# Weights' sums and low parts on VectorE, the keys' copy as a DMA, and matmuls of zeros ahead of the dense units

## The chip, the cores and the metric

The kernel runs on one core of one Trainium2 chip. The metric is device microseconds from the start to the end of one launch. TensorE multiplies 128x128 blocks into PSUM banks; VectorE (DVE in the profile), ScalarE (ACT) and GpSimd (POOL) are the elementwise engines; DMAs are issued by SyncE (SP), and a few by ScalarE. Each engine runs its own queue in order and waits on semaphores.

## The reference

Causal attention with decay (4 batches, 8 heads, 576 positions, head size 64), then two dense layers of 2304 tokens, 512 to 2048 to 512, one with the square of relu and one with elu between its matrices:

```
decay = cum[:, :, :, None] - cum[:, :, None, :]          # cum: running sum of log f
attn  = softmax(where(causal, -1e9, q @ k.T / 8 + decay))
x = (attn @ v) as 2304 x 512
x = relu(x @ w_in) ** 2 @ w_out                          # first layer (w1)
y = elu(x @ w_in2) @ w_out2                              # second layer (w2)
```

All is float32. The kernel splits each operand of a product into a high part, which a matmul takes in one pass, and a low part, the rest, and adds three matmuls: high by high, low by high, high by low.

## The kernel before

**Attention with dense units between.** Batch 0 runs with plain float32 operands (`Plain`); its A items (queries 0 to 255) come first for all heads, then the others. Batches 1 to 3 are loaded per head by `load_head` with part "F": ScalarE copies queries and keys to `qk1` (high parts), GpSimd makes the queries' low part in `qk2` and the keys' low part in the lower half of `qk1` (`ql`, `kl`, line 132), VectorE copies the keys' high part from `qk1` to `qk2` (`kh` is "v" for F, line 127), and a small DMA brings the rows of the decay (line 319). A head is loaded two items ahead of its use. While attention runs, `moe_step` puts pieces of six dense units (256 tokens each, half of the first layer's hidden units) between its steps; `fill` pays out credit for them and does nothing until the tokens of unit 0 and their weights are there. Weights come as raw 64-bit words, 16 tiles for the first units; `words` turns a tile into float32 with one ScalarE operation and four VectorE operations (lines 150 to 154), and a ScalarE copy and a subtraction give high and low parts.

**First layer's rest.** `first_layer(j)` runs blocks of 512 tokens in the order 3, 4, 0, 1, 2 (block 4 has 256). Per hidden chunk it makes 12 matmuls of 512 columns to `pH`, then relu (ACT), square (VectorE, line 573), high part (ACT, 574), low part (VectorE, 119), and 12 more matmuls to the four banks `O`, up to two chunks later. At a block's end VectorE adds `pr` and `operands` makes seven combinations of the block for the second layer with ACT, GpSimd (`yl` line 132, sums line 822) and VectorE, and stores them.

**Second layer.** It multiplies 2x2 blocks with seven products instead of eight, so the weights too need sums. `pair_weights(p)` prepares a pair of hidden chunks: four raw tiles through `words`, four sums of 128x256 (`add`, line 915) and seven high and low parts of 128x256 (`op`: ACT line 911, then `less` on GpSimd, line 132, tile `v`), and after a `yield` each, two high and low parts of 128x512 (ACT line 933, GpSimd line 132). Eight pairs exist. Pairs 0 to 3 are made while blocks 0, 1 and 2 of the first layer run (3, 4 and 5 of the 12 pieces), pair 4 in steps 4 to 6 of the second layer, pairs 5 to 7 from step 16 on (`w_at`: 2, 3, 2, 2 pieces after steps 18 to 21). A step is one block by one pair; steps 20 to 23 use pairs 4 to 7 for the first time. `first_product` makes seven products of six matmuls of 256 columns into four banks `P`, which ACT (line 995) and VectorE (lines 998, 1016) take out; then elu (1012, 1017 minimum; 1020 exp; 1021) and the low part (1024); `second_product` of the step before adds 24 matmuls of 512 columns.

The order of each engine's queue is fixed when the program is built, by a scheduler that lays the instructions out by its own estimates of time; so a change of engine also moves instructions that the code does not touch.

Of the kernel before, what the change touches and what calls it, by code (L numbers as in the profile page):

```python
# [10 lines left out]
F32 = mybir.dt.float32  # L11
F32R = mybir.dt.float32r
# [31 lines left out]

PLAIN_B = 4
CP = {'pA': 'a', 'pB': 'av', 'xA': 'a', 'xB': 'a'}
ENG = {'qk': 'aaa', 'ql': 'ppp', 'kh': 'pvv', 'kl': 'ppp', 'vh': 'ppp', 'vl': 'ppp', 'xl': 'pv'}
NORM = 'ap'
GL = 'pv'
SQ = 'appp'  # L50
# [4 lines left out]


OPS = 7
AUG0 = 2
AUG1 = 8
AUG_AT = 3  # L60
# [9 lines left out]
def f32(ap):  # L70
    return ap.bitcast(F32)
# [10 lines left out]
def attention_then_moe_kernel(ctx, tc, first, firstv, plain, qkv, aug0, f, w1, w2, out):  # L82
    nc = tc.nc
# [5 lines left out]
    const = pool(ctx, "const", 1, "left")  # L89
# [17 lines left out]
    def mask(ap, pat):  # L107
        nc.gpsimd.affine_select(out=ap, in_=ap, pattern=pat, compare_op=ALU.is_ge, fill=-8.0e9, base=0, channel_multiplier=1)
# [3 lines left out]
    seen = [None]  # L112
    trail = []

    def minus(eng, dst, x, hi):
        if eng == "p":
            less(dst, x, hi)
        else:
            nc.vector.tensor_tensor(dst, x, f32(hi), op=ALU.subtract)  # L119
# [11 lines left out]
    def less(dst, x, hi):  # L131
        nc.gpsimd.tensor_tensor(out=dst, in0=x, in1=f32(hi), op=ALU.subtract)  # L132
# [66 lines left out]
    ps_h = pool(un, "ps_h", 1, "left", space=PS)  # L199
# [37 lines left out]
    nc.gpsimd.memset(m4, 0.0)  # L237
    for k in range(2):
        mask(m4[64 * k:64 * k + 64, 224:288], [[-1, 64]])

    raws = {}

# [397 lines left out]
    def interleave(main, n_main, side, n_side):  # L640
        done = 0
        for i, _ in enumerate(main):
            while done * n_main < (i + 1) * n_side:
                if next(side, "end") == "end":
                    break
                done += 1
        return done
# [36 lines left out]
    started = [False] * NU  # L684
# [31 lines left out]
    for i in range(len(todo) + LAG):  # L716
        if i == AUG0:
            nc.sync.dma_start(out=aug[0:H], in_=aug0[0:H])
        if i == AUG1:
            nc.sync.dma_start(out=aug[H:], in_=aug0[H:])  # L720
        if i == AUG_AT:
            cpn = aug_split()
            aug_rows(slice(0, H), *cpn)
        if i == AUG1:
            aug_rows(slice(H, B * H), *cpn)
        while fetches and fetches[0][0] <= i + FETCH:
            fetch_head(*fetches.pop(0)[1:])
        if i == 0:
            for _ in range(5):
                stage()  # L730
        while loads and loads[0][0] <= i + AHEAD:
            load(*loads.pop(0)[1:])
        if i < len(todo):
            sg = soft(*todo[i])
            b, hp, kind, k = todo[i]
        else:
            sg = iter(())
        if i >= LAG:
            o = todo[i - LAG]
            og = outs(*o)  # L740
        else:
            o, og = None, iter(())
        for _ in range(W_AT[i] if i < len(W_AT) else 0):
            next(wl, None)
        n_moe = PACE[b] * COST[kind]
        n_out = {"A": 3, "4": 1, "B": 8}[o[2]] if o else 1
        n_steps = n_out + 1
        done = 0
        step = 0

        def fill():
            nonlocal done, step, credit
            step += 1
            trail.append(seen[0])
            credit += n_moe / n_steps
            while credit >= 1:
                credit -= 1
                if not moe_step():
                    credit = min(credit, 1.0)
                    break  # L760

        drain(sg)
        fill()
        for _ in og:
            fill()
        if o and o[2] in "AB" and o[3]:
            stored[o[0]] += 1
# [76 lines left out]
    def first_layer(j, nxt):  # L844
        t0, n = blocks[j]
        whole = t0 >= NU * CH
        x = xq.pop(j)
        if nxt is not None:
            fetch1(nxt)
        pr = xa.tile([128, NC, 512], F32, tag="xu", name="pr")  # L850
        if not whole:
            for i in range(n // CH):
                nc.sync.dma_start(out=pr[:, :, i * CH:(i + 1) * CH], in_=part[t0 // CH + i])
        po = [ps_O.tile([128, 512], F32, tag=f"O{c}", name=f"O{c}") for c in range(NC)]
        f0 = 0 if whole else 8

        def second_b(fc, gh, gl):
            for c in range(NC):
                mm3(po[c][:, 0:n], three([wout(1, fc, t, c) for t in range(2)], [gh[:, 0:n], gl[:, 0:n]]), fc == f0, fc == 15)

        pend, depth = [], DEPTH1 * 512 // n
        for fc in range(f0, 16):
            ph = h_tile()
            for c in range(NC):
                mm3(ph[:, 0:n], three([win(1, fc, t, c) for t in range(2)], [x[c][:, 0], x[c][:, 1]]), c == 0, c == NC - 1)
            g = relu2(ph, n, GL[1], "v")
            pend.append((fc, *g))
            if len(pend) > depth:
                second_b(*pend.pop(0))
            yield  # L870
        for p in pend:
            second_b(*p)
        for c in range(NC):
            y = pr[:, c, 0:n]
            if whole:
                nc.vector.tensor_copy(y, po[c][:, 0:n])
            else:
                nc.vector.tensor_tensor(y, po[c][:, 0:n], y, op=ALU.add)
        operands(j, pr)
        yield  # L880
# [23 lines left out]
    def pair_weights(p):  # L904
        wi = [w_tile([128, 4, 2, 256]), w_tile([128, 3, 2, 256])]
        wo = w_tile([128, 2, 2, 512])
        wp[p] = wi, wo

        def op(a, k):
            h, l = (wi[k // 4][:, k % 4, r] for r in range(2))  # L910
            nc.scalar.activation(out=h, in_=a, func=AF.Copy)  # L911
            less(l, a, h)

        def add(out, x, y, f):
            nc.gpsimd.tensor_tensor(out=out, in0=x, in1=y, op=f)  # L915

        ta, tb = (next_w() for i in range(2))
        a11, a12, a21, a22 = (t[:, c:c + 256] for t in (ta, tb) for c in (0, 256))
        op(a11, 0)
        op(a12, 5)  # L920
        op(a22, 4)
        add(a22, a21, a22, ALU.add)
        add(a21, a11, a21, ALU.subtract)
        add(a11, a22, a11, ALU.subtract)
        add(a12, a12, a11, ALU.subtract)
        op(a22, 3)
        op(a21, 2)
        op(a11, 1)
        op(a12, 6)
        yield  # L930
        for i in range(2):
            t = next_w()
            nc.scalar.activation(out=wo[:, i, 0], in_=t, func=AF.Copy)
            less(wo[:, i, 1], t, wo[:, i, 0])
            yield

    def fetch2(j, ks):
# [133 lines left out]
    ask_w()  # L1071
    wl2 = chain(pair_weights(p) for p in range(8))
    interleave(first_layer(0, 1), 9, wl2, 3)
    interleave(first_layer(1, 2), 9, wl2, 4)
    fetch2(4, range(0, 2))
    for i, _ in enumerate(first_layer(2, None)):
        if i in (3, 4, 5, 6, 7):
            next(wl2)
    fetch2(4, range(2, 3))
    fetch2(3, range(0, 6))  # L1080
# [73 lines left out]
```

## Time and profile before

| | us |
|---|---|
| median of 3 runs | 1055.4 (1054.61 to 1058.65) |
| profiled execution, its own time | 1054.71 |
| its span | 1052.7 |
| PE busy in the span | 1010.2 (96%) |
| DVE, ACT, POOL busy | 691.1, 545.8, 375.4 |

A matmul's end is modelled, so a matmul that waits for nothing seems to overlap the next one, and PE's busy share hides short pauses. Where starts matter, the distance from one matmul to the next is used. The column PEclk is the granted share of TensorE's clock, of 2.4 GHz; half of it is 1.2 GHz. Ahead of the first record of a change the column reads 1.00.

### The profile page before, as it was taken

To read this page: it belongs to the slowest core of one execution; us is meant where nothing else is said; L and a number is where in the kernel's file an instruction comes from. 1 tells how busy PE (TensorE), PEld (TensorE's weight loads), DVE (VectorE), ACT (ScalarE), POOL (GpSimd) and SP (SyncE) were. 2 spreads that over 40 slices of the span, in tenths; PEclk is the share of its full clock that TensorE was granted. 3 is DMA by queue.
4 is the path that set the end of the run, shared out by engine and by line. 5 is a ranking of instruction groups with operands and counts; after the bars stand their busy time and mean duration, and the time that the engine had idled before them with its cause. 6 is when DMAs were issued, how large, how long until landed. Compare 5 with 4: busy or idle time off the path is not lost.

```text
span 1052.7 us, 17378 instructions
## 1 busy us (share of the span) xinstructions
PE 1010.2 (96%) x6272; PEld 889.1 (84%) x6272; DVE 691.1 (66%) x1462; ACT 545.8 (52%) x1218; POOL 375.4 (36%) x400
## 2 busy tenths in 40 slices
PE   5899999999999999999999997999999999999998
PEld 3577788999999988889988775898988888899987
DVE  5993587776776548845467858695555878655554
ACT  4865688877886634424343434454334555333331
POOL 3556587576774300012144565440000445000000
PEclk9999999999999999999999999999999999999999
DMA  8843444543431074442645545625315365444502
GB/s 248 240 145 134 153 138 142 181 137 128 160 120 45 33 253 138 122 138 103 201 142 204 193 158 178 225 85 196 132 48 180 124 217 166 134 151 122 169 21 80
DMA packets 71960, 154.91 MB, mean 147 GB/s; under 512 B 8932, under 2 KB 34276, under 8 KB 71844
## 3 DMA queue, kind: packets, MB, share of 16 engines
q1 hardware_dynamic: 71812, 153.75, 44.8%
q8 instruction: 49, 0.80, 0.3%
q14 instruction: 35, 0.29, 0.1%
q10 hardware_dynamic: 64, 0.07, 0.0%
HBM read 115.15 MB, written 39.22 MB: 147 GB/s over the span
## 4 chain that ended last, share of the span: by engine, by line
PE 59%; issue 16%; DVE 12%; POOL 5%; ACT 4%; DMA 3%; SPq 0%; POOLq 0%; ACTq 0%; DVEq 0%
PE O L183 18%; PE pH L183 9%; PE P L183 8%; PE o L183 6%; PE ph L183 6%; PE pt L405 4%; PE pv L412 3%; DVE wt L153 2%; POOL v L132 2%; PE s L337 2%; PE s L338 2%; DVE wt L151 1%; POOL wt L915 1%; DVE wt L152 1%; PE pv L409 1%
## 5 line engine op out<-in xcount | busy, mean ns | idle before, releaser
L183 PEld LDWEIGHTS P<-xu,v 128*128 128x128 f32 x1536 | 200.3, 189 | 12.9 <-ACT hs L995 2.7
L183 PE MATMUL P<-xu,v 128*128 128x256 f32 x1536 | 203.5, 283 | 3.2 <-ACT hs L995 2.5
L183 PE MATMUL O<-v,gh 128*128 128x512 f32 x576 | 172.5, 395 | 0.6 <-ACT gh L966 0.5
L132 POOL TENSOR_TENSOR v<-wt,v 128x256 fp32r<-128x256 f32 (+1 forms) x72 | 72.5, 1015 | 211.7 <-ACT v L911 155.9
L183 PE MATMUL pH<-xu,w 128*128 128x512 f32 (+1 forms) x672 | 140.7, 360 | 0.0
L183 PEld LDWEIGHTS pH<-xu,w 128*128 128x128 f32 x672 | 114.0, 188 | 20.1
L183 PE MATMUL O<-gh,w 128*128 128x512 f32 (+1 forms) x448 | 122.8, 363 | 5.1 <-ACT gh L574 5.1
L183 PEld LDWEIGHTS O<-v,gh 128*128 128x128 f32 x576 | 103.4, 189 | 19.0 <-ACT gh L966 0.7
L995 ACT ACTIVATE hs<-P 128x256 f32<-128x256 f32 x128 | 47.9, 380 | 114.1 <-PE P L183 113.7
L183 PE MATMUL O<-v,gl 128*128 128x512 f32 x288 | 104.2, 394 | 0.5 <-DVE gl L988 0.5
L183 PEld LDWEIGHTS O<-gh,w 128*128 128x128 f32 x448 | 79.7, 189 | 19.9 <-ACT gh L574 6.2
L132 POOL TENSOR_TENSOR qk<-raw,qk 64x704 fp32r<-64x704 f32 (+1 forms) x48 | 78.9, 1643 | 20.4 <-ACT qk L123 15.2
L183 PE MATMUL O<-gl,w 128*128 128x512 f32 (+1 forms) x224 | 80.4, 365 | 3.9 <-DVE gl L119 3.9
L998 DVE TENSOR_TENSOR hs<-P,hs 128x256 f32<-128x256 f32 x96 | 40.4, 421 | 64.3 <-PE P L183 62.6
L132 POOL TENSOR_TENSOR yl<-pr,yh 128x512 fp32r<-128x512 f32 x18 | 24.7, 1371 | 158.7 <-ACT yh L815 108.2
L183 PE MATMUL o<-gh,w 128*128 128x256 f32 x384 | 76.6, 292 | 1.2 <-DVE xB L437 1.2
L150 ACT ACTIVATE wt<-wraw 128x512 f32<-128x512 f32 x57 | 38.2, 671 | 61.6 <-DMA wraw<-in_w_dram 38.6
L574 ACT ACTIVATE gh<-g 128x512 fp32r<-128x512 f32 (+1 forms) x80 | 46.8, 585 | 43.0 <-DVE g L573 39.1
L183 PE MATMUL ph<-xu,w 128*128 128x256 f32 x480 | 67.2, 287 | 1.3 <-DMA xu<-x 1.0
L1024 DVE TENSOR_TENSOR gl<-g,gh 128x512 fp32r<-128x512 f32 x64 | 47.3, 738 | 28.4 <-ACT gh L966 27.9
L573 DVE TENSOR_TENSOR g<-g 128x512 f32<-128x512 f32 (+1 forms) x56 | 45.4, 810 | 28.3 <-ACT g L569 28.2
L183 PEld LDWEIGHTS O<-v,gl 128*128 128x128 f32 x288 | 53.3, 188 | 11.6 <-DVE gl L988 0.8
(151 smaller groups left out, 2122.7 us busy)
## 6 DMA issues: line engine op xcount, KB each, us to landing
xu<-x SPq DMA_DIRECT2D x66, 512.0 KB
wraw<-in_w_dram SPq DMA_DIRECT2D x57, 512.0 KB
raw<-in_qkv_dram SPq DMA_DIRECT2D x24, 800.0 KB
x<-yh SPq DMA_DIRECT2D x31, 256.0 KB
x<-yl SPq DMA_DIRECT2D x31, 256.0 KB
x<-xs SPq DMA_DIRECT2D x16, 320.0 KB
xu<-x SPq DMA_DIRECT2D x16, 256.0 KB
raws_w<-in_w_dram SPq DMA_DIRECT2D x7, 512.0 KB
```

The source lines that it names most:

```text
L132: nc.gpsimd.tensor_tensor(out=dst, in0=x, in1=f32(hi), op=ALU.subtract)
L150: nc.scalar.activation(out=f32(t), in_=f32(hi), func=AF.Abs)
L153: nc.vector.scalar_tensor_tensor(t, hi, -0x40000000, t, op0=ALU.bitwise_and, op1=ALU.bitwise_or)
L183: nc.tensor.matmul(out=dst, lhsT=l, rhs=r, start=first and i == 0, stop=last and i == n - 1, skip_group_check=skip)
L337: nc.tensor.matmul(out=dst, lhsT=qk1[:, q0:q0 + 128], rhs=qk1[:, QW + j0:QW + j0 + n], start=first, stop=False)
L405: seen[0] = nc.tensor.transpose(dst, src, ident[:, c0:c0 + 128])
L412: seen[0] = nc.tensor.matmul(out=dst, lhsT=hh[2][:, J, :], rhs=hl[i], start=first and i == 0, stop=last and i == 1)
L573: (nc.vector if sq == "v" else nc.gpsimd).tensor_tensor(out=g[:, 0:n], in0=g[:, 0:n], in1=g[:, 0:n], op=ALU.mult)
L574: nc.scalar.activation(out=gh[:, 0:n], in_=g[:, 0:n], func=AF.Copy)
L995: nc.scalar.activation(out=o, in_=x, func=AF.Copy)
L998: nc.vector.tensor_tensor(o, y, x, op=ALU.add)
L1024: nc.vector.tensor_tensor(hl[i][1], gs[i], f32(hl[i][0]), op=ALU.subtract)
```

## The change

- `add` and the two `less` in `pair_weights` go from GpSimd to VectorE: per pair 4 sums and 7 low parts of 128x256, and 2 low parts of 128x512.
- Of the 12 pieces of pairs 0 to 3, block 1 gets 3 in place of 4, block 2 gets 6 in place of 5, the first at its first chunk.
- The keys' high part of batches 1 to 3 is copied from `qk1` to `qk2` by a DMA on SyncE's queue ("d"); the branch was there already.
- VectorE zeroes a tile of 128x128 at the start, and TensorE multiplies zeros into the units' bank `h` (256 columns each): 60 at once, and after each step of attention until unit 0 begins, 2 or 3 behind the last attention matmul, 59 in all.

```diff
-ENG = {'qk': 'aaa', 'ql': 'ppp', 'kh': 'pvv', ...}
+ENG = {'qk': 'aaa', 'ql': 'ppp', 'kh': 'pvd', ...}
...
+WARM, FILL, FILL_TO = 60, 2, 14
...
+    zero = const.tile([128, 128], F32R, name="zero")
+    nc.vector.memset(f32(zero), 0.0)
+    idle = ps_h.tile([128, 512], F32, tag="h", name="idle")
+
+    def busy(n):
+        for _ in range(n):
+            nc.tensor.matmul(out=idle[:, 0:256]..., lhsT=zero, rhs=zero.unsqueeze(1).broadcast_to([128, 2, 128]), start=True, stop=True)
+
+    busy(WARM)
...
+            went = False
             while credit >= 1:
                 credit -= 1
                 if not moe_step():
                     credit = min(credit, 1.0)
                     break
+                went = True
+            if not started[0] and not went and i < FILL_TO:
+                with tc.issue_after(seen[0].ins):
+                    busy(FILL + (step == 1))
...
         def op(a, k):
             h, l = (wi[k // 4][:, k % 4, r] for r in range(2))
             nc.scalar.activation(out=h, in_=a, func=AF.Copy)
-            less(l, a, h)
+            minus('v', l, a, h)
 
         def add(out, x, y, f):
-            nc.gpsimd.tensor_tensor(out=out, in0=x, in1=y, op=f)
+            nc.vector.tensor_tensor(out, x, y, op=f)
...
-            less(wo[:, i, 1], t, wo[:, i, 0])
+            minus('v', wo[:, i, 1], t, wo[:, i, 0])
...
-    interleave(first_layer(1, 2), 9, wl2, 4)
+    interleave(first_layer(1, 2), 9, wl2, 3)
     fetch2(4, range(0, 2))
     for i, _ in enumerate(first_layer(2, None)):
-        if i in (3, 4, 5, 6, 7):
+        if i in (0, 3, 4, 5, 6, 7):
             next(wl2)
```

Line numbers after the change are 13 to 18 higher from line 245 on. TensorE's queue at the start of the program, before (`s` scores, `pt` transposed weights of attention, `pv` their product with values):

```order
L333 MATMUL s<-rawA 128x256 x6
L405 MATMUL pt<-ident,ea 128x128 x4
L333 MATMUL s<-rawA 128x256 x2
L405 MATMUL pt<-ident,ea 128x128 x2
L409 MATMUL pv<-ea,rawA 64x256
L409 MATMUL pv<-ea,rawA 64x128
L405 MATMUL pr<-ident,rb 128x128 x2
```

The same place after the change (`idle` is the bank that the zeros go to):

```order
L250 MATMUL idle<-zero 128x256 x60
L346 MATMUL s<-rawA 128x256 x2
L250 MATMUL idle<-zero 128x256 x3
L346 MATMUL s<-rawA 128x256 x2
L250 MATMUL idle<-zero 128x256 x3
L346 MATMUL s<-rawA 128x256 x2
L418 MATMUL pt<-ident,ea 128x128
L346 MATMUL s<-rawA 128x256 x2
L418 MATMUL pt<-ident,ea 128x128 x2
L250 MATMUL idle<-zero 128x256 x2
```

The zeros stand ahead of the first scores and between the steps that follow. SyncE's queue where heads of batch 1 are loaded, before (319 decay rows, 448 a store of attention's result, 251 a head's fetch, 593 a unit's tokens):

```order
L319 DMA qk_1440<-aug 4x1280
L319 DMA qk_1704<-aug 4x1280
L448 DMA x_0_70<-xs 128x2x320
L251 DMA raw<-in_qkv_dram 128x1600
L593 DMA xu<-x_0_70 128x2x256
```

After (335 is the new copy of keys):

```order
L332 DMA qk_1562<-aug 4x1280
L335 DMA qk_1562<-qk_1561 64x576
L332 DMA qk_1826<-aug 4x1280
L461 DMA x_0_70<-xs 128x2x320
L335 DMA qk_1826<-qk_1825 64x576
L264 DMA raw<-in_qkv_dram 128x1600
```

The second copy stands behind a store and ahead of a head's fetch. VectorE's queue from the minimum of step 22 on, before (151 to 154 are `words`):

```order
L1012 TENSOR_SCALAR g<-hs 128x512
L1016 TENSOR_TENSOR hs<-hs 128x256
L1021 SCALAR_TENSOR_TENSOR g<-g,hs 128x512
L1024 TENSOR_TENSOR gl<-g,gh 128x512
L998 TENSOR_TENSOR hs<-P,hs 128x256
L1017 TENSOR_SCALAR g<-hs 128x512
L151 TENSOR_SCALAR wt<-wt 128x512
L998 TENSOR_TENSOR hs<-P,hs 128x256
```

The second half of the same step after the change (122 with `v` is a low part of a weight, 933 a sum of weights, 1042 and 1016 are 1024 and 998 of before):

```order
L1039 SCALAR_TENSOR_TENSOR g<-g,hs 128x512
L122 TENSOR_TENSOR v_10040<-wt,v_10040 128x256
L933 TENSOR_TENSOR wt<-wt 128x256
L1042 TENSOR_TENSOR gl<-g,gh 128x512
L933 TENSOR_TENSOR wt<-wt 128x256
L122 TENSOR_TENSOR v_10039<-wt,v_10039 128x256
L933 TENSOR_TENSOR wt<-wt 128x256
L122 TENSOR_TENSOR v_10039<-wt,v_10039 128x256
L933 TENSOR_TENSOR wt<-wt 128x256
L122 TENSOR_TENSOR v_10039<-wt,v_10039 128x256
L1016 TENSOR_TENSOR hs<-P,hs 128x256
```

Pair 7's sums and low parts now stand in VectorE's queue between a step's elu and the next addition.

## Rows read from the trace of the kernel before

**Rows 1.** Windows by stage: length, busy (count) per engine, granted clock, DMA share, GB/s.
```profile
12.70:24.00 11.30, 11.29 (x33) 7.94 (x33) 6.83 (x24) 7.12 (x20) 3.51 (x4) 1.00 0.84 259
24.00:60.00 36.00, 30.64 (x132) 18.80 (x132) 34.06 (x91) 28.89 (x78) 18.51 (x21) 0.95 0.86 240
...
120.00:220.00 100.00, 96.03 (x729) 89.66 (x728) 76.81 (x233) 83.09 (x208) 72.89 (x79) 1.00 0.45 149
...
600.00:680.00 80.00, 70.45 (x350) 57.38 (x349) 56.77 (x80) 34.64 (x67) 46.26 (x42) 1.00 0.59 210
...
820.00:900.00 80.00, 76.22 (x460) 67.44 (x459) 67.09 (x114) 43.13 (x93) 36.38 (x39) 0.98 0.55 183
```

**Rows 2.** Chain that ended last: start, us, what.
```profile
141.27 2.87 PE ph L183 x24
...
404.19 2.76 PE O L183 x12
```

**Rows 3.** Groups by form, 600 to 680 us: two that TensorE waits in.
```profile
L183 PE MATMUL O<-gh,w 128*128 128x512 f32 x72 | 22.5, 400 | 5.1 <-ACT gh L574 5.1
...
L183 PE MATMUL O<-gl,w 128*128 128x512 f32 x36 | 14.3, 411 | 3.9 <-DVE gl L119 3.9
```

**Rows 4.** Groups by form, 820 to 900 us: all matmuls.
```profile
L183 PE MATMUL P<-xu,v 128*128 128x256 f32 x295 | 40.1, 286 | 3.2 <-ACT hs L995 2.5 <-DVE hs L998 0.6
L183 PE MATMUL O<-v,gh 128*128 128x512 f32 x112 | 33.1, 406 | 0.6 <-ACT gh L966 0.5
L183 PE MATMUL O<-v,gl 128*128 128x512 f32 x53 | 18.0, 395 | 0.0
```

**Rows 5.** Groups by form, whole run: GpSimd on the weights.
```profile
L132 POOL TENSOR_TENSOR v<-wt,v 128x256 fp32r<-128x256 f32 x56 | 51.0, 921 | 158.3 <-ACT v L911 155.9 <-PE pH L183 2.4
...
L915 POOL TENSOR_TENSOR wt<-wt 128x256 f32<-128x256 f32 x32 | 27.5, 860 | 1.3
...
L132 POOL TENSOR_TENSOR v<-wt,v 128x512 fp32r<-128x512 f32 x16 | 21.5, 1344 | 53.4 <-ACT v L933 53.4
```

**Rows 6.** VectorE by line: ns least/median/most, first and last start.
```profile
L1016 DVE TENSOR_TENSOR hs<-hs x32: 411/424/1502, 688.8 to 1019.1; 128x256 f32<-128x256 f32 x32
L153 DVE SCALAR_TENSOR_TENSOR wt<-wraw,wt x57: 668/692/1793, 24.3 to 890.3; 128x512 int32<-128x512 int32 x57
L119 DVE TENSOR_TENSOR w<-wt,w x16: 681/684/694, 385.3 to 447.9; 128x512 fp32r<-128x512 f32 x16
L127 DVE CAST qk<-qk x24: 442/480/1923, 87.4 to 318.1; 64x576 fp32r<-64x576 f32 x24
```

**Rows 7.** VectorE's groups by form, 600 to 680 us.
```profile
L119 DVE TENSOR_TENSOR gl<-g,gh 128x512 fp32r<-128x512 f32 x9 | 8.6, 953 | 5.4 <-ACT gh L574 5.4
```

**Rows 8.** VectorE's groups by form, 820 to 900 us.
```profile
L1024 DVE TENSOR_TENSOR gl<-g,gh 128x512 fp32r<-128x512 f32 x14 | 11.3, 811 | 5.8 <-ACT gh L966 5.6
```

**Rows 9.** Timeline in block 2: start, us, instruction, idle before it.
```profile
653.55 0.69 DVE L153 SCALAR_TENSOR_TENSOR wt<-wraw,wt 128x512 int32<-128x512 int32 x1
654.16 0.68 DVE L573 TENSOR_TENSOR g<-g 128x512 f32<-128x512 f32 x1
...
654.88 0.63 ACT L574 ACTIVATE gh<-g 128x512 fp32r<-128x512 f32 x1 [0.95 <-DVE g L573]
...
655.57 1.20 PE L183 MATMUL O<-gh,w 128*128 128x512 f32 x4 [2.40 <-ACT gh L574]
```

**Rows 10.** Timeline about the stall of step 21.
```profile
869.95 1.50 DVE L1016 TENSOR_TENSOR hs<-hs 128x256 f32<-128x256 f32 x1
...
873.13 1.65 PE L183 MATMUL P<-xu,v 128*128 128x256 f32 x6 [2.53 <-ACT hs L995]
```

**Rows 11.** Chain of 126 to 142 us: a store of 320 KB.
```profile
129.57 2.30 DMA x<-xs
```

**Rows 12.** TensorE's timeline, first 70 us.
```profile
12.71 5.46 PE L333 MATMUL s<-rawA 68*128 68x256 f32 x12 [12.71 <-DMA wraw<-in_w_dram]
...
23.98 1.13 PE L333 MATMUL s<-rawA 68*128 68x256 f32 x4
```

More of the change, by code (lines that the diff above doesn't have):

```diff
@@ L46 @@
 CP = {'pA': 'a', 'pB': 'av', 'xA': 'a', 'xB': 'a'}
-ENG = {'qk': 'aaa', 'ql': 'ppp', 'kh': 'pvv', 'kl': 'ppp', 'vh': 'ppp', 'vl': 'ppp', 'xl': 'pv'}
+ENG = {'qk': 'aaa', 'ql': 'ppp', 'kh': 'pvd', 'kl': 'ppp', 'vh': 'ppp', 'vl': 'ppp', 'xl': 'pv'}
 NORM = 'ap'
@@ L239, in attention_then_moe_kernel @@
         mask(m4[64 * k:64 * k + 64, 224:288], [[-1, 64]])
+    zero = const.tile([128, 128], F32R, name="zero")
[3 more added lines that the diff above has]
+        for _ in range(n):
+            nc.tensor.matmul(out=idle[:, 0:256].rearrange("p (a b) -> p a b", a=2), lhsT=zero, rhs=zero.unsqueeze(1).broadcast_to([128, 2, 128]), start=True, stop=True)
+    busy(WARM)
     raws = {}
```

## The prediction

> **What bounds the kernel now.** I read first the windows by stage, for each engine's busy time and the clock; then the chain that ended last, for the pace of matmuls that wait for nothing; then the groups by form in the two late stretches where TensorE waits, and VectorE's and GpSimd's groups there; last the timelines about single stalls.
>
> TensorE is the bound nearly everywhere. Twelve matmuls of 512 columns in a row take 2.76 us and 24 of 256 columns 2.87 us [rows 2]: 0.230 and 0.1196 us each. What a stretch loses is its length less its matmuls at this pace. In 820 to 900 us there are 295 of 256 and 165 of 512 columns [rows 4]: 35.3 + 38.0 = 73.3 of 80 us, 6.7 lost. In 600 to 680 us TensorE's two large groups of waits are for the high part of g by ScalarE, 5.1 us, and for its low part by VectorE, 3.9 us [rows 3]: 9.0 us lost at least. In 120 to 220 us its busy count is 96.0 of 100 [rows 1], so at least 4 are lost. At the start it does nothing until 12.71 us, since the first scores wait for a load, and then runs without a gap at half the rate: twelve scores take 5.46 us, 0.455 each, and four 1.13 us at 23.98, 0.28 each with the modelled end [rows 12]. In 24 to 60 us VectorE is busy 34.06 of 36 us and the DMA engines 0.86 [rows 1]; the front is theirs, not TensorE's.
>
> Both late stretches have VectorE late while GpSimd works. VectorE's own clean durations are 0.42 us for 128x256 and 0.68 us for 128x512; the same lines have 1.50 and 1.79 us as their most [rows 6]. The low part of g has a mean of 0.953 us in 600 to 680 [rows 7] and 0.811 in 820 to 900 [rows 8], against 0.684 for a low part of the same shape in a stretch with no such neighbour [rows 6].
>
> **The weights' sums and low parts.** GpSimd loses 56 x 0.921 + 32 x 0.860 + 16 x 1.344 = 51.0 + 27.5 + 21.5 = 100 us [rows 5], 12.5 us for each of eight pairs. VectorE gets (7 + 4) x 0.42 + 2 x 0.68 = 6.0 us a pair, 48 us in all, at the durations of [rows 6]. That is less than half, and what GpSimd's part delayed on VectorE comes off it.
>
> In 600 to 680 us two pairs are made: VectorE is busy 56.8 us [rows 1], gets 12.0, and is back to about its clean durations for part of them (nine low parts alone give 9 x 0.27 = 2.4 us). So 56.8 + 12.0 - 2.4 = 66.4 of 80 us at the most; it has room. GpSimd's 46.3 us fall by 25 to 21. The stalls here are of one kind: [rows 9] show the square of a block's hidden chunk (line 573) starting at 654.16, right behind a step of `words` (line 153) on VectorE, then the high part, and TensorE 2.40 us late. Shorter operations in front of the square, of 0.68 us at the most where line 153 had up to 1.79 [rows 6], take most of it. But VectorE is in order, and the block gets six pieces in place of five: a sum or low part of 0.42 us, or a row of several, may stand in front of a square instead. If all of the 9.0 us went it would be -9 to -10; if the queue gave back all but a little, -2. I take -7, nearer to the first, since VectorE's load remains under 85%.
>
> In 820 to 900 us three pairs are made, 39 instructions on GpSimd, all that it does there [rows 1]. VectorE: 67.1 + 3 x 6.0 = 85.1 us of 80, less what the neighbour cost it. Line 1024 gives 14 x 0.13 = 1.8 us [rows 8]; 0.1 us for each of the 114 instructions there [rows 1] would be 11 us in all (an estimate). It leaves 74 of 80 us, 92%: it fits, with nothing to spare. TensorE's one large wait there is 2.53 us at 873.13, and it starts with one addition of 1.50 us at 869.95 in place of 0.42 [rows 10]; that addition, 1.1 us late, pushed what follows on ScalarE. It should go. The new rows of sums between a step's elu and the next addition (as VectorE's queue shows) cost perhaps a part of it elsewhere: eleven operations of 0.42 us are 4.6 us of a step that TensorE fills for 42 x 0.1196 + 24 x 0.230 = 10.5 us. From -5 (the 6.7 us lost fall to under two) to +5 (each of eleven operations in a step's way for half its length, twice). I take -1.5.
>
> The Trainium skill, page "SBUF — State Buffer", section "Who interferes with whom", says that a VectorE instruction with two inputs in SBUF contends with a GpSimd one that reads SBUF, by an exclusive lock under which the loser is blocked and not slowed. The trace agrees in kind: the 1.50 us [rows 10] are 0.42 and 1.08 more, and one GpSimd operation on weights takes 0.86 to 1.34 [rows 5]. By that rule alone all of the delay goes with the last GpSimd operation on weights; the rival B below is that case.
>
> Pairs 0 to 3 are also partly in blocks 0 and 1, and pair 4 in the first steps of the second layer; no window there loses much, and I put 0 for them (-1 to +1).
>
> **The keys' copy.** VectorE is rid of 24 copies at a median of 0.48 us and a most of 1.92 [rows 6], 12 to 18 us, between 87 and 318 us; in 100 us of this VectorE is busy 77% [rows 1]. A tenth of that on TensorE's path is 1.5 us. The DMA that takes its place moves 147 KB; the nearest row, a store of 320 KB, takes 2.30 us [rows 11]. It starts where the copy would, behind ScalarE's high part; in the same time GpSimd makes the low parts of queries and keys (its queue is 73% busy there [rows 1]), so these are ready no sooner, and a head is loaded two items ahead. It is hidden. If it were not, 24 heads at up to 2 us less the copy's 0.5 would give 36 us at the very worst; SyncE's queue has its stores between the copies, as its order shows, and one that waits for VectorE holds the copy back. I take -1.5, from -4 to +2.
>
> The Trainium skill, page "DMA: Bandwidth & Descriptors", section "Anatomy of one DMA", gives about 2 us of fixed cost to a DMA, whatever its size, which speaks against replacing a copy of half a microsecond. The 2.30 us here agree. By it the copy comes 1.5 us later per head; with the cover named above the sum stays.
>
> **The zeros.** 60 matmuls of 256 columns take 60 x 0.1196 = 7.2 us at the full rate, or twice this, 14.4, at the half. TensorE has nothing to do until 12.71 us, so they end between some 8.4 and 15.6 us if VectorE's zeroing lets them start by 1.2 (estimate). At worst they delay the first scores by 2.9 us. If the clock is up when these start, the stretch from 12.7 to 24, 11.29 us of TensorE at half rate without a gap [rows 1], is some 5.6 us of matmuls. But behind it stand VectorE, ScalarE and the loads, which fill 24 to 60. I take half: -2.5 (from -6 to +3). The other 59 are 7.1 us (14 at half rate); TensorE is busy 30.6 of the 36 us up to 60 [rows 1], so 5 us and more of waits are there to take them, and what does not fit is inside this range.
>
> **The sum.** Against the profiled execution's own 1054.7 us: front -2.5, attention -1.5, 600 to 680 -7, 820 to 900 -1.5, together -12.5: 1042.2, so 1042. The median of the runs is 1055.4, 0.7 above that execution.
>
> **The rivals.**
>
> B, GpSimd was all of it: every wait of 600 to 680 (9.0 to 11) and 5 of the 6.7 us of 820 to 900 go, the front gives 5. 1054.7 - 10 - 5 - 5 - 1.5 = 1033, and 1031 with 2 to 3 us of attention more. For it: the long values of [rows 6] and the stall of [rows 10]. Against: VectorE is in order, and [rows 9] show a wait behind a VectorE operation of its clean 0.69 us.
>
> C, the queue takes it back: VectorE's added 12 us stand ahead of squares and low parts, or the weights' fetch sets the pace, and 600 to 680 gives only 2, the front 1.5, attention 1: 1050. For it: [rows 9]. Against: a sum of 0.42 us is shorter than the delay that it replaces.
>
> D, VectorE becomes the bound in 820 to 900: each piece of a pair now waits on VectorE for ScalarE's high part, with a step's additions out of PSUM queued behind it. Eight pairs with four such waits of 0.6 us, in line, are 19 us; with the gains elsewhere kept (7 and 1.5 + 1.5) it comes to 1054.7 + 19 - 10 = 1064. It decides as soon as VectorE's sum there goes above TensorE's 10.5 us a step. For it: 92% at the best and 85.1 of 80 us without relief. Against: VectorE's low parts of g wait 5.8 us for ScalarE there today [rows 8], and sums can fill such gaps.
>
> E, the zeros push the front: the first scores come 2.9 us late and the 59 others stand in the way for 7 of their 14 us at half rate; with the later gains of 10 (7, 1.5 and 1.5) it is 1054.7 + 2.9 + 7 - 10 = 1054.6, no change. For it: no cold stretch here shows that the clock rises on such matmuls. Against: TensorE waits for nothing else in the first 12.7 us.
>
> **How the numbers follow.** 1042 and its neighbours (1037 to 1047) have 0.48, B 0.18, C 0.16, D 0.10, E 0.08. This kernel's runs can tell 0.5%, 5.3 us: 1050.1 to 1060.7 is no change. A and B are faster, and half of C, with 0.01 of E: 0.75. The rest of C and most of E are no change, 0.14, and D with a little of these slower, 0.11. The range that leaves out some D and the ends of B is 1031 to 1055.
>
> **What would show it.** The low part of g at 0.7 us in both stretches, and no addition of line 1016 (1034 then) above 0.6; waits for the high and low part of g in 600 to 680 under 3 us together; VectorE at 65 and 74 of 80 us; granted clock 1.00 before the first scores and these at 0.28 us each; the copy's DMA done before the head's scores with no TensorE wait on it. Wrong would be: VectorE's share over 95% in 820 to 900 with ScalarE waiting for its sums (D), or the first scores after 15 us at the half clock (E).

## The result, and the profile after

The change makes the kernel faster: 1040.45 us (1037.57 to 1043.46, 4 runs) against 1056.63 (1054.61 to 1058.65, 4 runs), ratio 0.9847, interval 0.9811 to 0.9883. The profiled execution took 1037.57 us, its span is 1035.7; before, 1054.71 and 1052.7. So the two profiles differ by 17 us.

The windows by stage of the changed kernel, with the columns of [rows 1], which they answer:

```profile
12.70:24.00 11.30, 11.30 (x38) 8.78 (x39) 5.08 (x17) 4.96 (x14) 2.20 (x3) 0.55 0.92 274
24.00:60.00 36.00, 34.71 (x195) 24.75 (x193) 34.38 (x90) 29.58 (x76) 20.34 (x22) 1.00 0.83 239
...
120.00:220.00 100.00, 96.99 (x728) 89.65 (x728) 67.85 (x221) 81.97 (x209) 70.85 (x81) 1.00 0.53 166
...
600.00:680.00 80.00, 78.60 (x415) 67.21 (x415) 67.14 (x118) 38.97 (x75) 23.53 (x16) 1.00 0.55 198
...
820.00:900.00 80.00, 79.52 (x497) 71.35 (x496) 68.64 (x148) 42.11 (x91) 0.00 (x0) 1.00 0.58 195
```

The changed kernel is 11 to 17 us ahead in the two late stretches, so they do not hold the same work as before, and counts alone mislead. At the pace of [rows 2] the matmuls of 600 to 680 us (239 of 512 and 111 of 256 columns before, 259 and 156 after, by the groups by form) fill 68.2 us before and 78.2 after: TensorE's loss falls from 11.8 to 1.8 us. In 820 to 900 us (179 and 318 after) they fill 79.2 us, and the loss falls from 6.7 to 0.8.

VectorE has 34 instructions more in 820 to 900 us and is busy only 1.5 us longer, but only 28 sums and low parts of weights fall in this window, where GpSimd made 39 in it before. A window of the same length in which VectorE makes all 39:

```profile
805.00:885.00 80.00, 79.52 (x504) 71.71 (x503) 73.70 (x165) 46.40 (x102) 0.00 (x0) 1.00 0.54 185
```

With the whole of the new work VectorE is busy 73.7 us, and TensorE is as full as in the other window. From 12.7 to 24 us the granted clock is 0.55: half, for most of the stretch, although the zeros ran before.

TensorE's groups by form in 600 to 680 us, the two of [rows 3]:

```profile
L186 PE MATMUL O<-gh,w 128*128 128x512 f32 x72 | 22.3, 395 | 0.0
...
L186 PE MATMUL O<-gl,w 128*128 128x512 f32 x36 | 14.0, 397 | 0.0
```

The 9.0 us of waits are gone. VectorE's lines after the change, least, median and most in ns, as in [rows 6] (1034 was 1016, 156 was 153); first the additions:

```profile
L1034 DVE TENSOR_TENSOR hs<-hs x32: 414/419/426, 677.8 to 1002.1; 128x256 f32<-128x256 f32 x32
```

And the third step of `words`:

```profile
L156 DVE SCALAR_TENSOR_TENSOR wt<-wraw,wt x57: 677/685/1726, 28.1 to 876.5; 128x512 int32<-128x512 int32 x57
```

No addition of this line is stretched any more: its most fell from 1502 to 426 ns. Line 156 still has a most of 1726, where other GpSimd work runs. VectorE's groups by form in 820 to 900 us, with the low part of g that was 811 ns [rows 8]:

```profile
L1039 DVE SCALAR_TENSOR_TENSOR g<-g,hs 128x512 f32<-128x512 f32 x16 | 11.0, 687 | 1.9 <-ACT g L1038 1.8
L1042 DVE TENSOR_TENSOR gl<-g,gh 128x512 fp32r<-128x512 f32 x16 | 11.0, 686 | 0.9 <-ACT gh L984 0.7
L156 DVE SCALAR_TENSOR_TENSOR wt<-wraw,wt 128x512 int32<-128x512 int32 x10 | 6.9, 686 | 0.1
```

All are at their clean durations. In 600 to 680 us they are not, since GpSimd still works on the blocks' low parts and differences there:

```profile
L122 DVE TENSOR_TENSOR gl<-g,gh 128x512 fp32r<-128x512 f32 x8 | 6.9, 866 | 0.8 <-ACT gh L587 0.7
```

0.953 went to 0.866 us only [rows 7], and yet no matmul waits for it. One new wait ends at 676 us, in the changed kernel's timeline there:

```profile
672.63 1.29 POOL L840 TENSOR_TENSOR pr<-pr 128x512 f32<-128x512 f32 x1 [1.08 <-DVE yl L122]
672.92 1.28 DVE L1030 TENSOR_SCALAR g<-hs 128x512 f32<-128x512 f32 x1
...
674.24 0.63 ACT L1038 ACTIVATE g<-g 128x512 f32<-128x512 f32 x1 [3.52 <-DVE g L1030]
...
675.77 0.62 ACT L984 ACTIVATE gh<-g 128x512 fp32r<-128x512 f32 x1
...
676.44 2.12 PE L186 MATMUL O<-v,gh 128*128 128x512 f32 x8 [1.40 <-ACT gh L984]
```

A minimum with a single input took 1.28 us in place of 0.42, while GpSimd computed a difference (line 840), and TensorE came 1.40 us late behind it. That is the same kind of disturbance, from the GpSimd work that the change left.

Where the 17 us are, by the start of the same instruction in the two profiles: ScalarE's 25th relu of the first layer, the first one after the dense units of attention, starts at 383.2 before and 382.4 after (0.8 gained); VectorE's last addition to `pr`, the end of the first layer, at 661.0 and 650.0 (11.0, so 10.2 more); ScalarE's last instruction of line 983 (1001 after), near the end of the second layer, at 1041.5 and 1024.5 (17.0, so 6.0 more).

These are single executions, and the first figure is not to be relied on: in the profiles of the runs below the 25th relu starts anywhere from 378.9 to 388.7 us, and at 388.7 with the weights' part alone, which changes nothing in attention's code. The other two hold. From the 25th relu to the last addition to `pr` it takes 277.0 to 277.8 us in the three profiles with the weights on GpSimd (before, `zeros_only`, `keys_only`) and 267.3 to 268.2 in three with them on VectorE (the changed kernel, `weights_only`, `no_zeros`); from there to the end of the span 390.1 to 391.7 and 385.7 to 387.0 (389.9 once below, in `warm80`).

### The profile page after: what moved, and what is told of

Its sections match the earlier page's. It is cut to its first block, busy times and chain, and to the rows that moved or that the text cites. A ratio compares the mean times of both kernels' runs of the same rounds, so it can differ in the third digit from the quotient of the medians.

```text
span 1035.7 us, 17605 instructions
## 1 busy us (share of the span) xinstructions
PE 1020.5 (99%) x6391; PEld 903.5 (87%) x6391; DVE 683.1 (66%) x1543; ACT 547.4 (53%) x1218; POOL 275.0 (27%) x296
## 4 chain that ended last, share of the span: by engine, by line
PE 81%; DVE 9%; DMA 3%; POOL 2%; ACT 2%; issue 2%; POOLq 0%; ACTq 0%; DVEq 0%; SPq 0%
PE O L186 29%; PE P L186 16%; PE pH L186 11%; PE o L186 6%; PE ph L186 5%; PE pt L418 4%; PE pv L425 3%; PE s L350 2%; DVE wt L156 2%; PE s L351 2%; PE s L346 1%; DMA x<-yl 1%; PE pv L422 1%; DVE wt L157 1%; POOL qk L135 1%
## 5 line engine op out<-in xcount | busy, mean ns | idle before, releaser
L186 PE MATMUL O<-v,gh 128*128 128x512 f32 x576 | 169.2, 393 | 1.4 <-ACT gh L984 1.4
L186 PE MATMUL O<-v,gl 128*128 128x512 f32 x288 | 101.0, 393 | 0.0
L135 POOL TENSOR_TENSOR qk<-raw,qk 64x704 fp32r<-64x704 f32 (+1 forms) x48 | 75.7, 1578 | 21.0 <-ACT qk L126 15.7
L1038 ACT ACTIVATE g<-g 128x512 f32<-128x512 f32 x64 | 40.2, 629 | 54.8 <-DVE g L1030 32.9
L984 ACT ACTIVATE gh<-g 128x512 fp32r<-128x512 f32 x72 | 45.4, 631 | 35.4 <-DVE g L1039 28.6
L186 PEld LDWEIGHTS ph<-xu,w 128*128 128x128 f32 x480 | 60.8, 190 | 1.6 <-DMA xu<-x 1.1
```

The lines of the kernel that those rows point to most:

```text
L186: nc.tensor.matmul(out=dst, lhsT=l, rhs=r, start=first and i == 0, stop=last and i == n - 1, skip_group_check=skip)
L984: nc.scalar.activation(out=gh, in_=g, func=AF.Copy)
L1038: nc.scalar.activation(out=gs[i], in_=gs[i], func=AF.Exp)
```

## The experiments

All ran beside runs of the kernel before. An edit is shown against the changed kernel, unless the text says otherwise.

**The parts one by one.** Only the weights' part (the keys' copy back on VectorE, no zeros), only the zeros, only the keys' copy, and all but the zeros:

```diff
weights_only, against the changed kernel (the tile of zeros goes too, here and in no_zeros):
-ENG = {... 'kh': 'pvd' ...}
+ENG = {... 'kh': 'pvv' ...}
-    busy(WARM)
-                    busy(FILL + (step == 1))
no_zeros, against the changed kernel:
-    busy(WARM)
-                    busy(FILL + (step == 1))
zeros_only, against the kernel before:
+    busy(WARM)
+                    busy(FILL + (step == 1))
keys_only, against the kernel before:
-ENG = {... 'kh': 'pvv' ...}
+ENG = {... 'kh': 'pvd' ...}
```

> Only the weights' sums and low parts on VectorE, with the new places of the pieces; the keys' copy stays on VectorE and there are no zeros. Theory 1 (the late stretches carry the whole gain, since GpSimd's neighbourhood and its slow chain go): 15 to 17 us faster than before, the same as the whole change. Theory 2 (the terms of the prediction: 8.5 from the weights, 4 from the rest): 8 to 9 us faster, and the whole change is then 4 to 8 us better than this run.

Measured: 1042.2 us, ratio 0.9862 (0.9836 to 0.9888). That is 14.5 us of the 16 by the ratio (12 to 17), and 12.7 by the two medians (1054.87 before). It is a little under the 15 to 17 of theory 1, but the late stretches carry nearly the whole gain, and the 8 to 9 us of theory 2 lie outside the interval.

> Only the 60 + 59 matmuls of zeros are added to the kernel before. Theory 1 (the first unit begins earlier, but the steps of attention end no earlier): within 2 us of before; the relu of the first unit 3 to 4 us earlier, batch 1's masks at 100 us no earlier. Theory 2 (a warm start is kept): 2 to 4 us faster. Theory 3 (the zeros stand in the way): 2 to 5 us slower.

Measured: 1055.7 us, ratio 1.0005 (0.9986 to 1.0023): between 1.5 us faster and 2.4 slower. The first unit's relu starts at 61.0 us in place of 63.7, and nothing of it is seen in the time, as theory 1 has it.

> Only the keys' high parts of batches 1 to 3 by a DMA. Theory 1: 1 to 3 us faster, all of it between 100 and 380 us. Rival (the DMA's latency or its place in SyncE's queue sets when a head is ready): 0 to 3 us slower, with TensorE waiting for a qk DMA.

Measured: 1053.25 us, ratio 0.9984 (0.9963 to 1.0004). A gain of 1.7 us is likely and not proven. TensorE's waits in that profile name a copy of keys once, with 0.2 us; in the next run's profile once, with 0.3; in the changed kernel's never.

> The whole change without the zeros. Theory 1: within 2 us of the whole change (1040.5). Theory 2: 2 to 4 us slower than it. Theory 3: 2 to 5 us faster than it.

Measured: 1041.64 us, ratio 0.986 (0.9834 to 0.9887); the whole change has 0.9847. The zeros neither help nor harm by more than the measurement can tell.

**GpSimd as a neighbour.** Two theories were left for the weights' gain: that GpSimd's reading stretches VectorE's operations (N), or that the slow chain through GpSimd delays what comes behind it (Q). Two kernels give GpSimd work for which only its own later work waits:

```diff
pool_reads:
+    def again(h):
+        for c in range(0, h.shape[1], 128):
+            a = f32(h[:, c:c + 128])
+            nc.gpsimd.tensor_tensor(out=zero, in0=a, in1=a, op=ALU.subtract)
...
             minus('v', l, a, h)
+            again(h)
...
             minus('v', wo[:, i, 1], t, wo[:, i, 0])
+            again(wo[:, i, 0])
pool_writes, the same with:
+    def again(h):
+        nc.gpsimd.tensor_copy(zero[:, 0:2], f32(h[:, 0:2]))
+        for _ in range(h.shape[1] // 64):
+            nc.gpsimd.memset(f32(zero), 0.0)
```

> The whole change; then GpSimd subtracts each weight's high part from itself into the dead tile of zeros (two instructions per 128x256, four per 128x512), which nobody reads: GpSimd reads SBUF about as long as before, and nobody waits for it except its own next work. Theory N (neighbourhood: VectorE's operations with two SBUF inputs are blocked while GpSimd reads): VectorE's low parts of g rise above 0.8 us in the mean in 600 to 680 and 820 to 900 us, and 4 to 10 us of the gain are lost (1045 to 1050). Theory Q (the chain through GpSimd was what delayed the words and the high parts; the neighbourhood is small): within 2 us of the whole change.

Measured: 1049.37 us, ratio 0.9942 (0.9922 to 0.9962).

> As pool_reads, but GpSimd reads only two columns of the high part and then writes zeros into the dead tile, five memsets of 128x128 for 128x256 and nine for 128x512 (0.2 us each): about as busy, but writing. Theory N: VectorE's durations stay near the least (below 0.75 us for the low part of g) and the time within 2 us of the whole change. Rival to N (any GpSimd work nearby slows VectorE, or its queue delays GpSimd's other work): as slow as pool_reads.

Measured: 1040.92 us, ratio 0.9848 (0.9813 to 0.9883). The copy is one of the five and nine instructions, and the memsets are four and eight.

GpSimd is about equally busy in both, and reading costs 8.5 us where writing (with a read of two columns) costs nothing that can be seen; all ten runs with reads are slower than all four with writes. The windows of 600 to 680 and 820 to 900 us, columns as in [rows 1], first with reads:

```profile
600.00:680.00 80.00, 77.81 (x393) 64.60 (x392) 66.53 (x111) 35.57 (x67) 47.30 (x61) 1.00 0.56 202
820.00:900.00 80.00, 77.85 (x479) 68.50 (x478) 77.86 (x156) 43.70 (x97) 37.95 (x65) 1.00 0.54 184
```

With writes:

```profile
600.00:680.00 80.00, 78.08 (x410) 66.52 (x409) 64.98 (x115) 37.89 (x73) 50.65 (x122) 1.00 0.55 197
820.00:900.00 80.00, 79.28 (x493) 70.66 (x492) 70.41 (x153) 44.18 (x96) 39.00 (x138) 1.00 0.52 179
```

In 820 to 900 us GpSimd is busy 38 and 39 us; VectorE needs 77.9 us for 156 instructions beside reads, and 70.4 for 153 beside writes. A part of this is work, since 39 of the 156 are sums and low parts of weights and only 30 of the 153. The same length of the run with writes, moved to where it holds 39 too:

```profile
810.00:890.00 80.00, 79.28 (x497) 70.92 (x497) 72.75 (x163) 45.43 (x100) 44.54 (x159) 1.00 0.53 185
```

So about 5 of the 7.5 us are stretch. VectorE's groups by form in 820 to 900 us, with reads:

```profile
L122 DVE TENSOR_TENSOR v<-wt,v 128x256 fp32r<-128x256 f32 x21 | 11.9, 569 | 0.5 <-ACT v L934 0.5
...
L1049 DVE TENSOR_TENSOR gl<-g,gh 128x512 fp32r<-128x512 f32 x14 | 10.2, 730 | 0.0
...
L1041 DVE TENSOR_TENSOR hs<-hs 128x256 f32<-128x256 f32 x8 | 3.9, 488 | 0.0
```

And with writes:

```profile
L122 DVE TENSOR_TENSOR v<-wt,v 128x256 fp32r<-128x256 f32 x16 | 6.7, 416 | 0.5 <-ACT v L934 0.5
...
L1049 DVE TENSOR_TENSOR gl<-g,gh 128x512 fp32r<-128x512 f32 x15 | 10.2, 683 | 0.8 <-ACT gh L991 0.7
...
L1041 DVE TENSOR_TENSOR hs<-hs 128x256 f32<-128x256 f32 x7 | 2.9, 416 | 0.2 <-ACT hs L1020 0.2
```

Theory N holds in the time. It misses in one detail: in 820 to 900 us the low part of g rose to 0.730 and not above 0.8 us, and most of VectorE's forms are a little longer instead; in 600 to 680 us it is above 0.8 in both runs (0.844 and 0.864), as in the changed kernel, and tells nothing. The reads were cut in pieces of 128 columns; whether that is why was not tried. The Trainium skill, page "SBUF — State Buffer", section "Who interferes with whom", names the difference: a two-input VectorE instruction contends with GpSimd instructions that read SBUF, not with one that only writes. The pair of runs agrees, 1049.4 against 1040.9 us.

This shows that such reads cost 8.5 us; it does not show that they were the whole of the weights' gain. From the 25th relu to the last addition to `pr` the profile with reads takes 270.8 us and that with writes 267.5: of the 10 us that the change gained in this part, reads take back 3.

The low parts alone back on GpSimd, the sums on VectorE:

```diff
lows_pool:
-            minus('v', l, a, h)
+            less(l, a, h)
-            minus('v', wo[:, i, 1], t, wo[:, i, 0])
+            less(wo[:, i, 1], t, wo[:, i, 0])
```

> The whole change, but the low parts of the weights stay on GpSimd (72 of its 100 us) and only the sums are on VectorE. Theory N: most of the gain is lost, 1047 to 1052, as GpSimd still reads beside VectorE for 72 us. Theory Q: the low parts have nobody who waits soon, so the sums, on which the next sum and ScalarE's high parts wait, carry the gain: 1040 to 1044.

Measured: 1045.59 us, ratio 0.9894 (0.9856 to 0.9931), between the two. VectorE is stretched again (groups by form in 820 to 900 us):

```profile
L1042 DVE TENSOR_TENSOR gl<-g,gh 128x512 fp32r<-128x512 f32 x15 | 12.4, 829 | 1.5 <-ACT gh L984 1.4
...
L156 DVE SCALAR_TENSOR_TENSOR wt<-wraw,wt 128x512 int32<-128x512 int32 x10 | 9.5, 947 | 0.1
```

These are the values of before (811 ns [rows 8], and line 153, which is 156 now):

```profile
L153 DVE SCALAR_TENSOR_TENSOR wt<-wraw,wt 128x512 int32<-128x512 int32 x11 | 10.1, 922 | 0.2
```

And still some two thirds of the gain remain: of the 16 us this run gives up about 5 (its runs go from 1042.58 to 1048.39). Added up, VectorE's instructions of 820 to 900 us take some 11 us longer here than at the clean durations of their forms, and some 12 before (estimates from the groups by form). So moving the sums, with the smaller parts of the change, gave most of the gain and left the stretch nearly as it was: a stretched VectorE is not the whole cause, and theory Q has a part in it. ScalarE's waits for GpSimd before the change, from 400 to 1030 us (total, times, longest in us), show the chain:

```profile
ACT v L911 <- POOL wt L915: 16.5, 21, 1.7
...
ACT wt L150 <- POOL v L132: 5.6, 8, 1.6
```

The high parts waited 16.5 us in all for the sums, and the first step of `words` 5.6 us for low parts; with the low parts alone on GpSimd ScalarE has neither wait. How much of this reached TensorE was not measured.

**The places of the pieces.**

```diff
old_pieces:
-    interleave(first_layer(1, 2), 9, wl2, 3)
+    interleave(first_layer(1, 2), 9, wl2, 4)
-        if i in (0, 3, 4, 5, 6, 7):
+        if i in (3, 4, 5, 6, 7):
```

> The whole change, but the pieces of pairs 0 to 3 stand as before (four in block 1, five in block 2). If the engine is all that matters: within 2 us of the whole change. If the places matter: 3 to 6 us slower, lost in blocks 1 and 2 (560 to 660 us) where a square waits behind a row of sums.

Measured: 1039.37 us (1032.28 to 1040.52), ratio 0.9825 (0.9782 to 0.9869). No gain from the new places is seen. One of the four runs, the profiled one, was 6 to 8 us below the others, and in it the granted clock was full throughout. TensorE's timeline at the start of the changed kernel:

```profile
1.05 9.81 PE L250 MATMUL idle<-zero 128*128 128x256 f32 x60 [1.05 <-DVE zero L245]
12.56 1.37 PE L346 MATMUL s<-rawA 68*128 68x256 f32 x4 [1.71 <-DMA rawA<-ca]
13.37 1.20 PE L250 MATMUL idle<-zero 128*128 128x256 f32 x3
14.38 1.91 PE L346 MATMUL s<-rawA 68*128 68x256 f32 x4
```

And of this run:

```profile
1.05 9.36 PE L250 MATMUL idle<-zero 128*128 128x256 f32 x60 [1.05 <-DVE zero L245]
12.74 1.10 PE L346 MATMUL s<-rawA 68*128 68x256 f32 x4 [2.33 <-DMA wraw<-in_w_dram]
13.49 0.71 PE L250 MATMUL idle<-zero 128*128 128x256 f32 x3
14.08 1.13 PE L346 MATMUL s<-rawA 68*128 68x256 f32 x4
```

In both the zeros end some 2 us before the scores' data come. In the first the clock fell in or just after this gap (scores x4 in 1.91 us), in the second it didn't (1.13). The clock does not explain the 6 to 8 us by itself: the profile of `lows_pool` kept it too, over an equal gap, and has the middle time of its five runs.

**80 zeros, which fill the gap.** With the new places, with the old ones, with the old ones and no zeros between attention's steps, and with the old ones and the blocks' low parts and differences on VectorE as well:

```diff
warm80:
-WARM, FILL, FILL_TO = 60, 2, 14
+WARM, FILL, FILL_TO = 80, 2, 14
old_warm80: this and the edit of old_pieces
old_warm80_nofill: this, with
+WARM, FILL, FILL_TO = 80, 2, 0
old_warm80_yl: the edits of old_warm80 and
-            minus("pv"[n[0] % 2], l, y, h)
+            minus("v", l, y, h)
-            nc.gpsimd.tensor_tensor(out=out, in0=x, in1=y, op=ALU.subtract)
+            nc.vector.tensor_tensor(out, x, y, op=ALU.subtract)
```

> The whole change with 80 zeros at the start in place of 60. In the traces the 60 end at 10.1 to 10.7 us and the first scores come at 12.6 to 12.9, and in that gap the granted clock falls to half in four of six profiled executions; 20 more at 0.12 us fill it. Theory G (the gap loses the warm start): granted clock 1.00 from the zeros to 40 us, first unit's relu near 56 us in place of 60, and 3 to 4 us faster than the whole change: 1036 to 1038. Rival (zeros do nothing for the time, the low and high runs are chance): 1040 to 1042 at any clock. Rival (zeros delay the first scores): first scores after 13.2 us, 1041 to 1043.

Measured: 1039.52 us (1036.14 to 1043.41), ratio 0.9835 (0.9804 to 0.9867). The windows of its start:

```profile
10.00:12.60 2.60, 2.52 (x22) 2.32 (x20) 0.00 (x0) 0.00 (x0) 0.00 (x0) 1.00 1.02 392
12.60:24.00 11.40, 11.06 (x62) 8.68 (x63) 8.12 (x29) 8.59 (x26) 4.20 (x5) 1.00 0.76 220
24.00:60.00 36.00, 34.35 (x193) 24.17 (x192) 35.40 (x83) 28.48 (x71) 18.54 (x20) 1.00 0.95 241
```

The gap is filled, the clock is full, and the first unit's relu starts at 56.7 us in place of 60.0. But the 25th relu starts at 380.9 in place of 382.4: of 3.3 us only 1.5 are left in this pair of profiles, less than that start scatters from profile to profile, and 1 us of difference in the medians is less than the runs scatter. Theory G is right on the clock; its 1036 to 1038 us are not reached, and what a full clock at the start is worth stays open. In 24 to 60 us VectorE is busy 35.40 of 36 and the DMA share is 0.95.

> 80 zeros, and the pieces of pairs 0 to 3 in their places before the change. Theory G and places that cost nothing: 1032 to 1035, all runs near the single low one (1032.3) of the run with old pieces; 1 to 5 us better than with the new places. If the places are all the same: equal to the run with 80 zeros and the new places within 2 us.

Measured: 1036.74 us (1034.86 to 1039.66), ratio 0.9812 (0.9782 to 0.9842). It is 2.8 us below the run with the new places; the intervals overlap, so the places' price stays open.

> 80 zeros, old places, and none of the 59 zeros between the steps of attention. If these hold the clock in the waits of 24 to 60 us: the clock falls there in some executions (as it does at 40 us before the change) and 2 to 3 us are lost. If they only stand in the way: 1 to 3 us faster than with them.

Measured: 1035.53 us (1032.36 to 1036.94), ratio 0.9793 (0.9765 to 0.9821). In its profile the clock did fall (0.70 from 12.6 to 24 us, 0.91 from 24 to 60), although the 80 zeros left no gap ahead of the scores: without zeros between the steps it fell some 4 us into them. No loss of time is seen, so the zeros between the steps have not shown a use.

> 80 zeros, old places, and the blocks' low parts yl and differences (line 840) all on VectorE, so that GpSimd has nothing left from 400 us on. Theory N with TensorE already dense in 560 to 680 us: VectorE's durations fall to the least there (low part of g 0.69 us) but the time stays within 2 us, since no matmul waits there any more. If some GpSimd delay is still on the path: 2 to 4 us faster. If VectorE is too full: slower, with squares late.

Measured: 1034.68 us (1033.64 to 1035.77), ratio 0.9788 (0.9762 to 0.9814). All six of its runs are below all six with 80 zeros and the new places (1036.14 at the least). Against the run with old places alone the 2 us are within the intervals, so whether a GpSimd delay was still on the path stays open. VectorE's groups by form in 560 to 680 us, of this run:

```profile
L122 DVE TENSOR_TENSOR gl<-g,gh 128x512 fp32r<-128x512 f32 x16 | 10.9, 684 | 0.0
L586 DVE TENSOR_TENSOR g<-g 128x512 f32<-128x512 f32 x15 | 10.3, 686 | 3.1 <-ACT g L582 3.1
...
L840 DVE TENSOR_TENSOR pr<-pr 128x512 f32<-128x512 f32 x10 | 6.8, 682 | 0.0
```

With GpSimd gone, every form is at its least: the square of 128x512 took 1069 ns in the mean with 80 zeros and old places alone, and a difference takes 0.68 us here where GpSimd needs 1.54. This kernel has the lowest median of those run, though only 0.9 us below the run without zeros between the steps, and all of its runs are below all of the changed kernel's.

## Why the prediction was right, and where it was off

The forecast was 1042 us, 12.5 less than the profiled execution; measured are 1040.45, and 16 less by the medians. The side and the mechanism are right: the gain comes from the weights' work leaving GpSimd. That the sum lies within 2 us is in part luck, since it comes out of terms that are off in both directions.

- **600 to 680 us, -7.** Measured are -10.2 for the whole stretch from 383 to 661 us, at the outer end of the term (-9 to -10). Every wait for the parts of g in these blocks went. The cost that was weighed against the gain, rows of sums standing ahead of a square, was nothing that TensorE waited for; VectorE is busy 67.1 us where 66.4 were worked out.
- **820 to 900 us and the rest of the second layer, -1.5.** This is the term that was most mis-sized: -6.0 from 661 us to the end, past its outer end of -5. VectorE's load was forecast well: 74 of 80 us, and 73.7 in the window that holds all 39 sums and low parts; the relief was put at 11 us, and by the groups by form the 114 instructions of before took some 12 us longer, added up, than at the clean durations of their forms (an estimate). What failed is the price of that load. The rows of sums between a step's elu and the next addition were held to take back part of a possible -5, and no such cost is seen: TensorE's loss falls from 6.7 to 0.8 us. Rival D never comes near.
- **The weights together, -8.5.** Alone they give -14.5 by the ratio (12 to 17 us) and -12.7 by the medians. Rival B had the right late half: 10 and 5 us. The prediction held [rows 9] against B, as a wait behind a VectorE operation of its clean 0.69 us. The two steps of `words` ahead of that operation were not clean: GpSimd made two low parts from 651.62 us on, and they took 0.94 and 0.84 us in place of 0.42, so [rows 9] too has the neighbour in it:

```profile
651.62 1.61 POOL L132 TENSOR_TENSOR v<-wt,v 128x256 fp32r<-128x256 f32 x2
...
651.70 0.94 DVE L151 TENSOR_SCALAR wt<-wt 128x512 f32<-128x512 f32 x1 [2.02 <-ACT wt L150]
...
652.68 0.84 DVE L152 TENSOR_SCALAR wt<-wt 128x512 int32<-128x512 int32 x1
```

- **The front, -2.5.** Measured 0 with the zeros alone (1.5 us faster to 2.4 slower). The step that failed is "if the clock is up when these start": in the six profiles with 60 zeros they end at 9.8 to 10.9 us, the scores start at 12.6 to 12.9, and in four of the six, the changed kernel's among them, the clock falls in this gap or just behind it. The other reason is the one that the prediction gave and then only halved: even with the clock full until 60 us, VectorE and the loads fill that stretch, and of 3.3 us at the first unit 1.5 are left at the end of attention, which is within the scatter.
- **The keys' copy, -1.5.** Measured -1.7, with 0 in its interval. It is hidden but for one wait of TensorE of 0.2 to 0.7 us in seven of the eleven profiles with it. The section that the prediction cites beside it, "Anatomy of one DMA" on the page "DMA: Bandwidth & Descriptors" of the Trainium skill, gives its 2 us for DMAs that GpSimd issues, and SyncE issues this copy; how long one took was not read.
- Of the signs named ahead, the low part of g is at 0.69 us in 820 to 900 us but at 0.87 in 600 to 680, and the additions stay below 0.43. The column's 1.00 ahead of the first scores says nothing, since it reads so ahead of any record; the zeros' own pace does: 16 of them fall in 2 to 5 us and 28 in 7 to 10, so the clock was up before they ended. The scores at 0.28 us each were not there.

What stays open: how much of the weights' gain is neighbourhood and how much the chain through GpSimd, whether the new places cost 2 to 3 us, and what a full clock at the start is worth.

## What to carry to other kernels

A busy engine beside the critical one is not free when both read SBUF: price a move by what the neighbour's least and most durations say, line by line, and not by the moved work alone. Load on an engine that is not the bound is not yet a cost either: 73.7 of 80 us on VectorE cost TensorE nothing here. When two kernels are compared in a window of time, count first whether it holds the same work. Compare an operation's least, median and most before moving work; a most of three times the least, on one line and one shape, is the sign. A clock raised ahead of time can be lost before the first real work or soon behind it, and even when kept it is worth only what the stretch behind it can use.

## What the runs showed of the hardware

- GpSimd work that reads SBUF stretches VectorE, and about the same busy time spent almost only on writes doesn't: a low part of 128x256 took 569 against 416 ns in 820 to 900 us, and the kernel 1049.4 against 1040.9 us.
- It holds for a VectorE instruction with one input too: a minimum of 128x512 took 1.28 us beside a GpSimd difference, and 0.42 without. The section "Who interferes with whom" of the Trainium skill's page "SBUF — State Buffer" lists tensor_scalar among the operations that can, in a mode with two ports, block and be blocked; the row agrees.
- Zeros raised TensorE's clock (16 in 2 to 5 us, 28 in 7 to 10), and it was lost in or just behind a gap of some 2 us in one execution (0.55 from 12.7 to 24 us) and kept over a gap of like length in another (1.00).
- GpSimd's own reads vary as much: its subtraction of 128x128 took 398 ns at the least, 466 in the median and 2532 at the most. That VectorE is what stretches it was not tested.
